# Retention between the products of the first of four d_ff passes, instead of ahead of all products

## The chip, the cores and the metric

One core of one Trainium2 chip. Times are device microseconds of one execution; a kernel is run several times and the median is quoted. Engines: PE is TensorE, PEld its weight loads, DVE is VectorE, ACT is ScalarE, POOL is GpSimd, SP is SyncE, whose queue (SPq) issues nearly all DMAs.

A line of a profile's timeline reads: start and duration in us, engine, line of the program (L396), operation, what is written <- what is read, shapes, xcount. Brackets give the engine's idle time before it and what ended it; "<-issue" means that the profile shows no releaser. "Evacuation" is the copy or addition that takes a product's result out of PSUM, the accumulator memory.

## The reference

Retention (attention with a decay in place of the softmax) makes x, and a two-layer block with the activation `h * erf(softplus(h))` follows. Everything is float32, except the weights, which come as float64 and are rounded in the kernel.

```python
batch, n_heads, seq, head_dim = (8, 8, 576, 64)        # q, k, v
n_tokens, d_model, d_ff = (4608, 512, 2048)            # w_in: 512 x 2048, w_out: 2048 x 512

scores = scale * np.matmul(q, k.transpose(0, 1, 3, 2))
Dmat = np.where(rel >= 0, gamma[:, None, None] ** rel[None, :, :], 0.0)
attn_out = np.matmul(scores * Dmat, v)
x = attn_out.transpose(0, 2, 1, 3).reshape(B * S, H * D)

h = x @ w_in
sp = np.maximum(h, 0.0) + np.log1p(np.exp(-np.abs(h)))
return (h * erf(sp)) @ w_out
```

## The kernel before

It works in two parts. Part one goes through 40 pieces of up to 128 tokens (8 batches of five, the fifth of 64 tokens). Each piece has three stages on TensorE: transposes of q and k; scores; outputs, with a running state `kv` that carries earlier pieces of the batch. The result x goes to DRAM in nine chunks of 512 tokens. In the same part all 32 float64 weight tiles are rounded to float32, on ScalarE, VectorE and GpSimd in turn, and "sums" of weight blocks are made.

The sums are there because both matrix products are done with seven block products in place of eight (Strassen's method in Winograd's form): sums of blocks of the weights (S1 to S4, T1 to T4) and of x or g, seven products, sums of the results. One product in the text below is one call of `product` or `multiply1` for one group of columns: four float32 matmuls, eight matmul instructions in the trace.

```python
        for i in range(n_p + 2):                      # part one
            if i < n_p:
                transposes(i)
            if 0 <= i - 1 < n_p:
                scores(i - 1)
            if i >= 2:
                store((b * S + s0) // TCH)
                outputs(i - 2)
            round_weights(-(-len(todo) * (i + 1) // (n_p - 2)))
        store(n_ch)
    ...
    for c in range(n_ch):                             # part two, chunk by chunk
        for g in range(n_g):                          # four groups of d_ff
            middle_products(c, g)                     # S2, S3, S1
            if g > 0:
                finish_group(c, g - 1)
            if g + 1 < n_g:
                first_products(c, g + 1)              # A11, A12
            ...
            last_products(c, g)                       # S4, A22
            serf(c, g)
        ...                                           # 28 products by w_out, accumulated in PSUM over g
        load_x(c + 1)
        ...
```

The rounding of a weight tile is the same in both kernels:

```python
        nc.scalar.activation(a_f, high_f, AF.Abs)
        nc.scalar.mul(out=r_f, in_=low, mul=2.0**-52)
        nc.vector.tensor_scalar(...)                  # four VectorE operations
        ...
        nc.gpsimd.tensor_tensor(out=r_f, in0=high_f, in1=r_f, op=ALU.mult)
        nc.gpsimd.tensor_tensor(out=a_f, in0=a_f, in1=r_f, op=ALU.add)
        load_weights()
        if sums:
            sums(...)                                 # four VectorE adds; they wait for GpSimd
```

## Time and profile before

| | |
|---|---|
| time | 1186.71 us median of 3 runs (1184.98 to 1187.42) |
| part one, to the first product | 298 us, TensorE busy 217 us, clock 0.82 |
| part two | 889 us, TensorE busy 875 us, clock 1.00 |
| busy over the span | PE 92%, DVE 43%, ACT 34%, POOL 10% |

Read the table by halves. In part two TensorE is idle for 14 of 889 us, so little but fewer or cheaper products can help there. In part one it is idle for 81 of 298 us, and its clock is lowered. The lines that show this stand in the prediction.

### The profile page before, as it was taken

Reading aid. Unit: us, or ns where it says so; the run is one execution under the profiler, and the core shown is the slowest. Engines: PE = TensorE matmul, PEld = TensorE weight load, DVE = VectorE, ACT = ScalarE, POOL = GpSimd, SP = SyncE. Lnnn points to the kernel's source line nnn. Section 1 sums busy time; section 2 is a strip of 40 time slices with the busy share of each in tenths; the row PEclk is TensorE's granted clock in tenths of the full one; section 3 lists DMA queues with packets and bytes.
Section 4 is the critical chain, followed back from the end, with each engine's and each line's share of the span. In section 5 each row is a group of like instructions: output and inputs, shape, how many; then the busy total and the mean of one; then the engine's idle time right before and its main releaser. Section 6 shows DMA issues by size and latency. Waiting matters only on the chain.

```text
span 1186.5 us, 14961 instructions
## 1 busy us (share of the span) xinstructions
PE 1092.2 (92%) x6400; PEld 950.7 (80%) x6400; DVE 510.6 (43%) x721; ACT 403.2 (34%) x533; POOL 120.4 (10%) x110
## 2 busy tenths in 40 slices
PE   4778678876999999999999999999999999999998
PEld 3666567665888888888888888888888888888887
DVE  3766665664462164056045317315504622721540
ACT  3343344331361162055036016205404602520630
POOL 3544444341000000000000000000000000000000
PEclk8888887778999999999999999999999999999999
DMA  9878977972010000001001000100000000000000
GB/s 256 183 184 194 225 194 191 223 177 97 12 36 1 36 1 36 36 1 36 16 20 36 1 36 1 36 36 1 36 18 19 36 1 36 21 15 36 1 1 36
DMA packets 124818, 75.76 MB, mean 64 GB/s; under 512 B 113616, under 2 KB 113616, under 8 KB 122320
## 3 DMA queue, kind: packets, MB, share of 16 engines
q1 hardware_dynamic: 124608, 73.41, 24.1%
q10 hardware_dynamic: 144, 1.40, 0.3%
q8 instruction: 50, 0.82, 0.3%
q14 instruction: 16, 0.13, 0.0%
HBM read 55.92 MB, written 18.87 MB: 63 GB/s over the span
## 4 chain that ended last, share of the span: by engine, by line
PE 75%; DMA 7%; ACT 5%; DVE 5%; POOL 3%; issue 2%; SPq 1%; ACTq 0%; POOLq 0%; DVEq 0%
PE acc_a L362 21%; PE oa L432 20%; PE acc_g L362 10%; PE og L432 10%; PE acc_e L362 5%; ACT e L410 2%; PE s L245 2%; DMA raw_k<-in_k_dram 2%; DMA raw_q<-in_q_dram 2%; PE o L261 2%; DVE g L143 1%; PE oe L432 1%; DMA raw_v<-in_v_dram 1%; PE o L271 1%; POOL wraw L198 1%
## 5 line engine op out<-in xcount | busy, mean ns | idle before, releaser
L432 PE MATMUL oa<-wb,s 128*128 128x256 f32 x864 | 191.0, 379 | 0.7 <-ACT osb L477 0.7
L432 PEld LDWEIGHTS oa<-wb,s 128*128 128x128 f32 x864 | 164.1, 190 | 23.3 <-ACT osb L477 1.1
L362 PE MATMUL acc_a<-x,wa 128*128 128x256 f32 x576 | 138.0, 383 | 7.9 <-DMA x<-xd 7.9
L362 PE MATMUL acc_a<-xs,wa 128*128 128x256 f32 x576 | 136.1, 379 | 0.0
L362 PE MATMUL acc_g<-xs,wa 128*128 128x256 f32 x576 | 136.1, 379 | 0.0
L143 DVE TENSOR_TENSOR osb<-og,osb 128x512 f32<-128x512 f32 x18 | 12.5, 692 | 284.2 <-ACT osb L477 166.4
L362 PEld LDWEIGHTS acc_a<-x,wa 128*128 128x128 f32 x576 | 110.4, 192 | 23.2 <-DMA x<-xd 8.0
L432 PE MATMUL og<-wb,g 128*128 128x256 f32 x576 | 127.3, 379 | 0.0
L362 PEld LDWEIGHTS acc_a<-xs,wa 128*128 128x128 f32 x576 | 109.4, 190 | 14.9
L362 PEld LDWEIGHTS acc_g<-xs,wa 128*128 128x128 f32 x576 | 109.4, 190 | 14.9
L432 PEld LDWEIGHTS og<-wb,g 128*128 128x128 f32 x576 | 109.4, 190 | 14.9
L410 ACT ACT_TABLE_LOAD x72 | 92.4, 1283 | 67.5 <-DVE g L143 66.9
L143 DVE TENSOR_TENSOR g<-g,e 128x1024 f32<-128x1024 f32 x72 | 84.7, 1218 | 52.0 <-ACT e L410 52.0
L245 PE MATMUL s<-qT,kT 64*128 64x128 f32 (+1 forms) x640 | 58.7, 339 | 23.7 <-DVE sT L143 23.6
L245 PEld LDWEIGHTS s<-qT,kT 64*128 64x128 f32 (+1 forms) x640 | 49.7, 236 | 31.8 <-DVE sT L143 26.5
L432 PE MATMUL oa<-wb,g 128*128 128x256 f32 x288 | 67.5, 382 | 7.9 <-DVE g L143 7.9
L410 ACT ACTIVATE e<-g 128x1024 f32<-128x1024 f32 x72 | 72.1, 1049 | 1.0 <-DVE g L143 0.6
L410 ACT ACTIVATE e<-e 128x1024 f32<-128x1024 f32 x72 | 72.1, 1049 | 0.4
L432 PEld LDWEIGHTS oa<-wb,g 128*128 128x128 f32 x288 | 54.0, 190 | 18.5 <-DVE g L143 11.5
L362 PE MATMUL acc_e<-x,wa 128*128 128x256 f32 x288 | 68.4, 380 | 0.0
L394 DVE COPY g<-acc_a 128x512 f32<-128x512 f32 x36 | 24.9, 692 | 99.4 <-PE acc_a L362 99.4
L382 ACT COPY g<-acc_a 128x512 f32<-128x512 f32 x36 | 20.7, 576 | 137.0 <-PE acc_a L362 137.0
(58 smaller groups left out, 1167.3 us busy)
## 6 DMA issues: line engine op xcount, KB each, us to landing
xd<-xT SPq DMA_DIRECT2D x9, 1024.0 KB, 6.2
x<-xd SPq DMA_DIRECT2D x9, 1024.0 KB, 4.8
out_dram<-osb SPq DMA_DIRECT2D x18, 512.0 KB, 2.8
raw_q<-in_q_dram SPq DMA_DIRECT2D x32, 256.0 KB, 5.1
raw_k<-in_k_dram SPq DMA_DIRECT2D x32, 256.0 KB, 6.0
raw_v<-in_v_dram SPq DMA_DIRECT2D x32, 256.0 KB, 6.3
wraw<-in_moe_w_in_dram SPq DMA_DIRECT2D x16, 512.0 KB, 4.5
wraw<-in_moe_w_out_dram SPq DMA_DIRECT2D x16, 512.0 KB, 3.8
```

The costliest lines, as they stand in the source:

```text
L143: nc.vector.tensor_tensor(out=out, in0=in0, in1=in1, op=op)
L198: nc.gpsimd.tensor_tensor(out=r_f, in0=high_f, in1=r_f, op=ALU.mult)
L245: nc.tensor.matmul(ps[:n, e, p, :n], lhsT=t["kT"][r, p, :n], rhs=t["qT"][r, p, :n], start=True, stop=True)
L261: nc.tensor.matmul(o[e * D : (e + 1) * D, p, :n], lhsT=t["v"][:n, 2 * p + e, :], rhs=t["sT"][:n, e, p, :n], start=(p == 0), stop=(s0 == 0 ...
L271: nc.tensor.matmul(o[:, p, :n], lhsT=kept["state"][:, p, :], rhs=t["qT"][:, p, :n], start=False, stop=(p == NP - 1), skip_group_check=True,)
L362: nc.tensor.matmul(acc[:, j * TH : (j + 1) * TH], lhsT=wa[:, a, d, f : f + P], rhs=x[c][a][:, d, :], start=(start and j == 0 and d == 0), ...
L382: nc.scalar.copy(out=t["g1"][:, 0], in_=t["a"])
L394: nc.vector.tensor_copy(out=t["g2"][:, 1], in_=t["a"])
L410: nc.scalar.activation(t["e" + j], t["g" + j] if func == AF.Softplus else t["e" + j], func)
L432: nc.tensor.matmul(acc[:, tp, :], lhsT=left[:, j * TH + tp * P : j * TH + (tp + 1) * P], rhs=wb[:, a, g * GP + j, :], start=(start and g = ...
```

## The change

The intent is to fill part one's idle TensorE with products. The d_ff columns are taken in four passes, and each pass goes through all nine chunks, so that only a quarter of the weights is needed to begin. The retention stages of chunk n+2 run between the products of chunk n in the first pass. The weights of a pass are rounded one pass ahead, one tile per chunk. The price: outputs are sums over passes, so each chunk's partial output goes to DRAM and comes back, and x is loaded and its block sums are made in every pass.

```diff
-    wa = const.tile([P, 7, 2, D_FF // 2], FP32, name="wa")
-    wb = const.tile([P, 7, n_fp, OH], FP32, name="wb")
+    wpool = ctx.enter_context(tc.tile_pool(name="wpool", bufs=2))      # weights of two passes
+    od = [dram.tile([P, 2, 2, D_MODEL], FP32, tag="od", name="od") for _ in range(n_ch)]
...
+    def attend(upto):                       # the next retention stages, in order
+        while done[0] < min(upto, len(stages)):
+            of, i = stages[done[0]]
+            of(i)
+            done[0] += 1
...
+        def begin(self):
+            self.o = opool.tile([P, 2, 2, D_MODEL], FP32, tag="o", name="o")
+            if self.g > 0:
+                nc.sync.dma_start(out=self.o, in_=od[self.c])
...
+    order = [(g, c) for g in range(n_g) for c in range(n_ch)]
...
+    weigh_values(0)
+    while done[0] < stages_for(TCH):
+        attend(done[0] + 1)
+        if done[0] % 2 == 1 and rounded[0] < 7:
+            round_weights()
+    sums_x(0, 0)
+    def run(steps):                         # a retention stage behind every product
+        for _ in steps:
+            attend(done[0] + 1)
+    run(firsts[0].first())
+    run(firsts[0].middle())
+    run(firsts[0].last())
+    firsts[0].erf()
+    round_weights()
+    attend(stages_for(2 * TCH))
...
+    for b, nxt in zip(blocks[1:], blocks[2:] + [None]):
+        n = order.index((b.g, b.c))
+        if isinstance(b, First):            # products by w_in
+            seconds[n - 1].begin()
+            if n + 1 < n_s and order[n + 1][0] > 0:
+                load_x(*order[n + 1])
+            run(b.middle())                 # S2, S3, S1
+            firsts[n - 1].sums()
+            run(seconds[n - 1].first())     # B11, B21
+            run(b.last())                   # S4, A22
+        elif n + 2 < n_s:                   # products by w_out
+            f = firsts[n + 1]
+            steps = b.middle()              # T2, T3, T1
+            for step, _ in enumerate(steps):
+                attend(done[0] + 1)
+                if step == 0:
+                    f.erf()
+            if n + 2 < n_ch:
+                attend(stages_for((n + 3) * TCH))
+            sums_x(*order[n + 2])
+            run(nxt.first())                # A11, A12
+            f.multiply()
+            run(b.last())                   # B22, T4
+            round_weights()
...
```

Cut here: the constants (the decay by position is split in two factors, so the scaling of outputs is four operations a piece and not one), the classes First and Second with the same seven products as before, the scores in two PSUM tiles.

## The prediction

> **What bounds the kernel now.** I read the page's 40 slices first, then the busy time of the two halves, then the timeline inside each half. Three rows of the slices (TensorE busy in tenths, its granted clock in tenths, DMA busy in tenths) show two programs one after the other:
>
> ```profile
> PE   4778678876999999999999999999999999999998
> PEclk8888887778999999999999999999999999999999
> DMA  9878977972010000001001000100000000000000
> ```
>
> Ten slices of retention with TensorE part idle, its clock at 0.7 to 0.8 and the DMA nearly full; then thirty of the MoE block with TensorE full and the DMA empty. The busy time by stretch (columns PE, PEld, DVE, ACT, POOL, clock, DMA share, GB/s) gives the boundary, 298 us:
>
> ```profile
> 0.00:298.00 298.00, 216.95 (x2368) 184.00 (x2368) 172.26 (x262) 105.14 (x209) 120.42 (x110) 0.82 0.82 192
> 298.00:1187.00 889.00, 875.27 (x4032) 766.68 (x4032) 338.38 (x459) 298.01 (x324) 0.00 (x0) 1.00 0.06 21
> ```
>
> The second half is bound by TensorE: 875 of 889 us at clock 1.00, VectorE (DVE) 38% busy. The timeline there gives the unit of the whole argument, one product of eight matmul instructions, and the VectorE steps behind it:
>
> ```profile
> 600.71 1.89 PE L362 MATMUL acc_a<-xs,wa 128*128 128x256 f32 x8
> 602.44 1.89 PE L362 MATMUL acc_a<-x,wa 128*128 128x256 f32 x8
> 602.64 0.69 DVE L394 COPY g<-acc_a 128x512 f32<-128x512 f32 x1 [2.76 <-PE acc_a L362]
> 603.37 0.69 DVE L143 TENSOR_TENSOR g<-acc_g,g 128x512 f32<-128x512 f32 x1
> 604.17 1.89 PE L362 MATMUL acc_e<-x,wa 128*128 128x256 f32 x8
> 616.06 2.35 DVE L143 TENSOR_TENSOR g<-g,e 128x1024 f32<-128x1024 f32 x2
> ```
>
> Products start 1.727 us apart (600.71, 602.44, 604.17). 4032 / 8 = 504 products, so 504 x 1.727 = 870 us is the floor of that half, and only about 19 us of it is anything else. The first half, by contrast, waits: for q, k, v loads, for VectorE, and on a slow clock. Where it does run freely, near its end, the timeline shows what retention costs TensorE at full clock:
>
> ```profile
> 270.16 0.66 PE L232 MATMUL pt_q<-ident,raw_q 128*128 128x128 f32 x4
> 270.65 0.60 PE L232 MATMUL pt_k<-ident,raw_k 128*128 128x128 f32 x4
> 275.16 2.08 PE L245 MATMUL s<-qT,kT 64*128 64x128 f32 x16 [3.90 <-DVE sT L143]
> 281.05 1.11 PE L245 MATMUL s<-qT,kT 64*128 64x128 f32 x15
> 282.09 1.09 PE L261 MATMUL o<-sT,raw_v 128*64 128x128 f32 x16
> 283.11 1.16 PE L271 MATMUL o<-qT,state 128*128 128x128 f32 x8
> 284.20 0.69 PE L285 MATMUL kv<-raw_v,raw_k 128*64 128x64 f32 x16
> 298.10 3.78 PE L362 MATMUL acc_a<-x,wa 128*128 128x256 f32 x8 [7.86 <-DMA x<-xd]
> ```
>
> By starts, a full piece takes 0.49 + 0.56 + 1.04 + 1.02 + 1.09 + 0.61 = 4.8 us, against 298 / 40 = 7.4 us for a piece as it ran. The scores at 275.16, after a wait of 3.90 us, took 2.08 us where 1.11 is the full-clock time; the first product, after 7.86 us, took 3.78.
>
> **What the Trainium skill says.** "TensorE: Matmul & The Clock Gate", Part 1, has the clock fall to half after an idle window of about 3.4 us; the two pairs above agree (2.08 for 1.11, 3.78 for 1.89). So retention put between dense products should run at full clock. "ScalarE: Activation LUTs", What ACT_TABLE_LOAD costs, gives about 1283 ns for a load; this trace has 72 of mean 1283 ns, and the count stays 72. "VectorE: DVE Perf Modes", The TRN2 errata, gives (N+151)/0.96 ns for an fp32 tensor-tensor op; this trace agrees at 512 (691 to 692 ns). At 128 it gives 0.29 us, an estimate, for the new per-head scaling ops, of which this trace has none. "DMA: Bandwidth & Descriptors", Why small descriptors are slow, says small ones lose bandwidth; here 113616 of 124818 packets are under 512 B, almost all q, k, v, and the slices above are DMA-full while they load.
>
> **The change part by part.** The instruction counts come from the built program. TensorE's matmuls are the same in number and shape: 504 products, 40 pieces of retention. What changes is order.
>
> 1. Retention moves between the first pass's products. 32 full pieces x 4.8, less 8 x 1.09 for the pieces that start a batch and have no state product, plus 8 short pieces x about 2.9 (from their rows at 280.5 to 290) = 168 us of TensorE at full clock, in place of a 298 us stretch.
> 2. A start remains: the first chunk needs pieces 0 to 3 done and piece 4 transposed, with 7 of 32 weight tiles rounded beside them. In the trace before, piece 3's kv product ends near 47 us. The constants shrink from 2728 to 700 columns, about 1 MB less, but more weights are wanted early. I take 45 us, in which four of forty pieces (16 us of TensorE at full clock) get done.
> 3. So TensorE has 870 + 168 - 16 = 1022 us left after 45: 1067 us if nothing ever waits.
> 4. Between products 7 and 8 of the first chunk, three pieces must run without products between them. At 7.4 instead of 4.8 us a piece: +8 us.
> 5. VectorE gets heavier. Partial outputs are summed through DRAM: per chunk and later pass 7 adds of 0.69 us into the output tile; before, 7 such steps (4 of them on ScalarE) served four groups. The x sums, 4 x 0.69, run 36 times instead of 9. Per chunk of 14 products (24.2 us): 5 evacuations 3.5, two multiplies 2.4, sums 2.6, x sums 2.6, output adds 4.8 = 15.9 us, 66% busy. That fits, but VectorE works in order. From product T1's end: two adds, four x sums, one add, two multiplies, two adds = 0.72 + 0.69 + 2.54 + 0.70 + 2.37 + 1.42 = 8.4 us; TensorE next needs the last of these after five products, 8.6 us. Hardly covered: I put 0.2 us on each of 27 chunks, 5 us.
> 6. In 16 chunks of passes 2 and 3 (and in 8 of the first) one weight tile is rounded right at that point. Its four ops (0.43 + 0.43 + 0.69 + 0.43, about 2.1 us with gaps) go ahead of the copy that product S1 waits for: 8.5 + 2.1 + 0.7 = 11.3 us against 10.4 covered, about 1 us. In four of the 16 the tile's sums follow, and these wait for GpSimd (1.1 + 1.3 us) and then take 2.6 more: about 6 us. 12 x 1 + 4 x 6 = 36 us.
> 7. In the first pass a chunk has 24.2 + 4.4 pieces x 4.2 = 43 us of TensorE. VectorE has 15 + 4.4 x 3.0 (masks now in two ops of 0.69, scaling in four ops of 0.29, state add) + 3.8 for weights = 32 us, 75%. A retention stage is needed two products and one stage later, about 4.5 us, and VectorE's blocks of 2.4 to 2.75 us fit inside with little over. I put 2.5 us on each of 8 chunks and 4 us on the two with weight sums: 28 us.
> 8. Weight-load conflicts where the matmul shape changes, 240 times: the rows show gaps of 0 to 0.2 us only now and then. 8 us.
> 9. The end: no product is left to hide the last Softplus, Erf and multiplies behind, and the last partial output must come back by DMA (1 MB took 4.8 us for x). 6 us.
>
> DMA: a later chunk moves 1 MB x, 1 MB partials in, 1 MB out and at times 0.5 MB weights in 24 us, some 145 GB/s; the retention half ran 192 on average with small packets. Hidden, I expect.
>
> Sum: 45 + 1022 + 8 + 5 + 36 + 28 + 8 + 6 = **1158 us**, 2.4% faster.
>
> **The rivals.** First, TensorE stays full throughout (steps 5 to 8 nearly nothing): about 1085 to 1100. For it: ScalarE is below 40%, two accumulators alternate, and chunks already evacuate behind products without loss. Against: 75% of VectorE in strict order, where one late op stops TensorE. Second, VectorE becomes the real bound of the first pass: if scaling ops and GpSimd contention (the "wa" sums took 1113 ns instead of 692 beside GpSimd) bring it to 90%, the first pass costs 430 to 450 us and not 350 to 390; and once TensorE waits over 3 us its clock halves too. About 1190 to 1220. Third, DMA: the partial tile's load queues behind the reload of a weight buffer, which waits for GpSimd, and so arrives when product T2 is about to need its accumulator; 1 to 2 us on each of 27 chunks, +30 to 50 us. The trace speaks neither way.
>
> **Range and chances.** The certain part is 1067. The waits total 91 and rest on orderings that I walked by hand; I allow 40 to 140. **Predicted 1158, range 1105 to 1205.** The 2% line is at 1163, close above my number: faster 0.54, within 2% 0.39, slower 0.07.
>
> **What would show it.** Steps 1 and 3: clock near 1.0 and TensorE above 90% from about 50 us on; a transposition group of four about 0.5 us. Step 2: first "a" product near 45 us. Steps 5 and 6: TensorE idle before "a" products, released by VectorE, in bursts of 1 and 6 us that vanish in the last pass, which rounds no weights. Step 7: VectorE 70 to 80% in the first pass, and a pass of about 380 us. I am wrong if the first pass runs at a clock of 0.8, if later passes without rounding exceed 24.5 us a chunk, or if waits on DMA show up on VectorE.

## The result, and the profile after

The changed kernel took 1167.99 us (median of 4 runs, 1166.91 to 1172.49) against 1186.34 us of the kernel before in the same rounds. Ratios here are the mean time of one kernel's runs over that of the other's runs of the same rounds, so not quite the ratio of the medians: 0.9853, 95% interval 0.9825 to 0.9881. That is 1.5% faster, inside the predicted range, 10 us above the predicted number and on the other side of the 2% line.

The slices of the changed kernel's page (busy tenths of PE and DVE, PE's clock):

```profile
PE   6679999999999998998999799989998999999996
DVE  5756566666576575766566566666775565665654
PEclk8888999999999999999999899999999999999998
```

The slow retention half is gone: from the fourth slice on TensorE is nearly full, and from the fifth its clock is up, even while retention runs, to slice 14. Busy time by stretch (columns PE, PEld, DVE, ACT, POOL, clock, DMA share, GB/s); I cut at the first product, the second chunk's first product, the end of retention (just behind the ninth chunk's first product) and the end of rounding:

```profile
0.00:49.30 49.30, 28.21 (x256) 23.50 (x256) 28.55 (x54) 15.31 (x27) 18.91 (x22) 0.83 0.79 192
49.30:100.60 51.30, 39.33 (x356) 32.03 (x353) 28.74 (x57) 14.72 (x22) 13.47 (x12) 0.87 0.58 132
100.60:408.00 307.40, 304.97 (x2595) 253.52 (x2592) 199.79 (x411) 101.56 (x153) 44.90 (x41) 1.00 0.48 124
408.00:914.00 506.00, 469.24 (x2101) 403.57 (x2100) 328.26 (x503) 165.57 (x188) 42.73 (x36) 0.98 0.34 129
914.00:1165.10 251.10, 240.82 (x1104) 210.06 (x1102) 150.78 (x217) 74.97 (x78) 0.00 (x0) 0.99 0.33 122
```

In the third stretch, where retention and products are mixed, TensorE idles 2.4 of 307 us. It loses time in the first two (100 us, a third of it idle and the clock at 0.85) and in the fourth (37 us idle). The timeline inside the first pass shows mixed work at full clock, the retention stages as short as the fastest ones of before:

```profile
103.14 1.99 PE L371 MATMUL e<-x,wa 128*128 128x256 f32 x8
104.97 0.60 PE L243 MATMUL pt_q<-ident,raw_q 128*128 128x128 f32 x4
105.40 0.60 PE L243 MATMUL pt_k<-ident,raw_k 128*128 128x128 f32 x4
105.84 1.89 PE L371 MATMUL a<-xs,wa 128*128 128x256 f32 x8
```

The fourth stretch is best seen in one of its gaps. This is a chunk whose rounded tile completes a block, so that the four sums (`wa<-wa`, L91) follow the rounding:

```profile
544.28 1.89 PE L371 MATMUL a<-xs,wa 128*128 128x256 f32 x8
546.01 1.89 PE L371 MATMUL g<-xs,wa 128*128 128x256 f32 x8
547.15 0.43 DVE L201 TENSOR_SCALAR wraw<-wa 128x512 uint32<-128x512 uint32 x1
547.71 1.04 POOL L202 TENSOR_TENSOR wraw<-wraw 128x512 f32<-128x512 f32 x1 [22.42 <-issue]
548.83 1.27 POOL L203 TENSOR_TENSOR wa<-wa,wraw 128x512 f32<-128x512 f32 x1
550.14 2.62 DVE L91 TENSOR_TENSOR wa<-wa 128x512 f32<-128x512 f32 x4 [2.56 <-POOL wa L203]
552.67 0.68 DVE L396 COPY t<-a 128x512 f32<-128x512 f32 x1
553.41 3.78 PE L371 MATMUL a<-xs,wa 128*128 128x256 f32 x8 [5.51 <-DVE t L396]
```

Product S2 ended before 546.2, and S1 may only begin when VectorE has copied S2's result (L396). That copy takes 0.68 us, but it stands in VectorE's queue behind four sums, and the sums wait 2.56 us for GpSimd. TensorE idles 5.51 us, and then its clock is down: S1 takes 3.78 us where 1.89 is usual. In the stretch there are five such gaps (4.70, 5.51, 5.11, 5.51, 5.11 us), eleven of 0.33 us in chunks that round a tile without sums, and six of 0.25 to 1.62 us ahead of product T2. After 914 us, where no weights are left to round, the products follow each other without a gap until the last 30 us: 24.17 us a chunk, 14 x 1.727.

### The profile page after: what moved, and what is told of

Same layout as the page of the kernel before. It is cut to its first block, busy times and chain, and to the rows that moved or that the text cites. A ratio compares the mean times of both kernels' runs of the same rounds, so it can differ in the third digit from the quotient of the medians.

```text
span 1165.1 us, 15647 instructions
## 1 busy us (share of the span) xinstructions
PE 1082.6 (93%) x6400; PEld 922.7 (79%) x6400; DVE 736.1 (63%) x1240; ACT 372.1 (32%) x467; POOL 120.0 (10%) x110
## 5 line engine op out<-in xcount | busy, mean ns | idle before, releaser
L450 PE MATMUL a<-wb,s 128*128 128x256 f32 x864 | 208.1, 384 | 10.8 <-DVE o L91 10.8
L450 PEld LDWEIGHTS a<-wb,s 128*128 128x128 f32 x864 | 162.7, 191 | 37.2 <-DVE o L91 12.6
L371 PE MATMUL a<-xs,wa 128*128 128x256 f32 x576 | 147.4, 401 | 32.9 <-DVE t L396 31.4
L91 DVE TENSOR_TENSOR o<-a,o 128x512 f32<-128x512 f32 x108 | 74.4, 689 | 134.8 <-PE a L450 104.2
L371 PEld LDWEIGHTS a<-xs,wa 128*128 128x128 f32 x576 | 112.0, 199 | 56.1 <-DVE t L396 38.6
L371 PE MATMUL a<-x,wa 128*128 128x256 f32 x576 | 137.3, 381 | 0.0
L371 PE MATMUL g<-xs,wa 128*128 128x256 f32 x576 | 137.1, 381 | 0.0
L371 PEld LDWEIGHTS g<-xs,wa 128*128 128x128 f32 x576 | 108.2, 190 | 14.9
L371 PEld LDWEIGHTS a<-x,wa 128*128 128x128 f32 x576 | 108.1, 190 | 15.0
L91 DVE TENSOR_TENSOR t<-t,s 128x1024 f32<-128x1024 f32 x72 | 85.9, 1234 | 0.0
L91 DVE TENSOR_TENSOR t<-g,t 128x512 f32<-128x512 f32 x72 | 49.7, 690 | 43.9 <-PE g L371 42.6
```

The source lines that it names most:

```text
L91: nc.vector.tensor_tensor(out=out, in0=in0, in1=in1, op=op)
L371: nc.tensor.matmul(acc[:, j * TH : (j + 1) * TH], lhsT=weights["wa", self.g][:, a, d, j * P : (j + 1) * P], rhs=x[self.g, self.c][a][:, d, :],
L450: nc.tensor.matmul(acc[:, tp, :], lhsT=left[:, j * TH + tp * P : j * TH + (tp + 1) * P], rhs=weights["wb", self.g][:, b, j, :], start=(sta ...
```

## The experiments

Nine kernels ran, all with correct results. Each was timed beside the kernel before on its own chip (1185.76 to 1186.44 us there), in three rounds; "the change" below is 1168 us.

**Sums later.** Only the four sums move, one chunk on, behind the evacuation of product T2:

```diff
         if sums:
-            sums(*(w[:, i] for i in range(7)))
+            late.append(lambda: sums(*(w[:, i] for i in range(7))))
+            if g == 0:
+                finish_weights()                # the first pass's own weights: as before
...
                 if step == 0:
                     f.erf()
+                    finish_weights()
```

> Only the four sums of a finished weight block move, from behind the rounding (where they wait for GpSimd and stand ahead of the copy that product S1 needs) to one chunk later, behind the evacuation of product T2. Theory (in-order VectorE, not its load, makes the waits): the five TensorE gaps of 4.7 to 5.5 us before an S1 product and the half-clock product behind each (up to 1.9 us more) go: 26 + 8 = 34 us, so about 1134 us; the gaps of 0.33 us stay. Rival (VectorE is the bound of the later passes, so the same work stalls TensorE wherever it stands): the gaps reappear elsewhere, 1155 us or more.

It took 1130.99 us (1130.5 to 1134.05), ratio to before 0.9542 (0.9514 to 0.9571): 37 us less than the change, for the same work in another order. The fourth stretch, 408 to 914 us, in this run:

```profile
408.00:914.00 506.00, 492.52 (x2250) 424.76 (x2250) 347.54 (x530) 178.61 (x201) 41.80 (x36) 1.00 0.36 135
```

VectorE is now busier in this stretch (347.5 us against 328.3, since more chunks fit in it), and TensorE idles 13.5 us in place of 36.8. None of the five long gaps is left (nor one of 1.84 us at 297 us, in the first pass), and the clock is 1.00; the gaps of 0.33 us stay, as expected, and so do those before T2. So VectorE's load was not the bound; the place of the sums was.

**Reload behind the other loads.** Only the issue of the next weight load moves on SyncE's queue:

```diff
-        load_weights()
+        if g == 0:
+            load_weights()
...
                 load_x(*order[n + 1])
+            if len(words) < 4:
+                load_weights()
```

> Only the reload of the weight buffer moves on the SyncE queue: behind the loads of the partial tile and of x, not ahead of them. Theory (the queue stands still for the reload, which waits for GpSimd, and the partial tile comes 2 to 5 us late): the seven gaps of 0.25 to 1.6 us before T2 products go, 7 us in all, about 1161 us. Rival (the DMA is simply full in those microseconds): they stay, 1168 us.

(The change's trace has six such gaps, not seven; I had miscounted.) It took 1159.35 us (1157.99 to 1160.34), ratio 0.9772 (0.9749 to 0.9795): 8.6 us less. In the change, SyncE's queue stands until GpSimd has let go of the buffer that is to be reloaded, and the load of the partial tile (`o<-od`) is behind it:

```profile
581.17 1.28 POOL L203 TENSOR_TENSOR wb<-wb,wraw 128x512 f32<-128x512 f32 x1
582.48 0.55 SPq L170 DMA_DIRECT2D wraw<-in_moe_w_in_dram  x1
583.12 0.55 SPq L444 DMA_DIRECT2D o<-od  x1
590.35 0.69 DVE L91 TENSOR_TENSOR o<-a,o 128x512 f32<-128x512 f32 x1 [3.80 <-DMA o<-od]
591.10 1.99 PE L450 MATMUL a<-wb,s 128*128 128x256 f32 x8 [1.62 <-DVE o L91]
```

In the run with the reload behind, the same load of the same chunk is issued while GpSimd has not even begun, and VectorE's addition comes straight behind the sums of g:

```profile
577.70 0.60 SPq L445 DMA_DIRECT2D o<-od  x1
579.37 1.04 POOL L202 TENSOR_TENSOR wraw<-wraw 128x512 f32<-128x512 f32 x1 [30.05 <-issue]
585.18 0.69 DVE L91 TENSOR_TENSOR s<-t,s 128x512 f32<-128x512 f32 x1
585.78 0.68 DVE L91 TENSOR_TENSOR o<-a,o 128x512 f32<-128x512 f32 x1
```

The six gaps before T2 products in the fourth stretch are gone. The DMA had room; the queue's order was the cause.

**The change without its overlap.** All retention runs first, and x comes from DRAM in the first pass too:

```diff
+    attend(len(stages))
+    load_x(0, 0)
     sums_x(0, 0)
+    load_x(0, 1)
...
-            if n + 1 < n_s and order[n + 1][0] > 0:
+            if n + 1 < n_s:
```

> The change without its overlap: all retention runs first, x goes through DRAM also for the first pass, then the four passes, with rounding a pass ahead as in the change. Theory (the overlap is what gains, the passes cost): first product near 290 us, then 870 us of products, six waits for weight sums of 7 us each, 12 us of small gaps and 9 us at the end: about 1225 us, slower than both. Rival (the gain of the change is the rounding taken out of the retention half): about 1180 us or less.

It took 1226.57 us (1224.28 to 1229.7), ratio 1.0342 (1.0313 to 1.037). The total is as the theory had it, but two of its terms were off and cancelled. The first product began earlier, and a gap came that I had not counted, behind the rounding and sums of the first pass's last tile:

```profile
256.56 3.50 PE L371 MATMUL a<-x,wa 128*128 128x256 f32 x8 [8.29 <-DMA x<-xd]
286.46 3.75 PE L371 MATMUL a<-xs,wa 128*128 128x256 f32 x8 [11.54 <-DVE xs L91]
```

So there are three amounts. With seven weight tiles and not 32 rounded beside it, smaller constants and its stages in their new order, retention took 257 us to the first product and not 298; no run separates these three. The rest of this version, passes and all, took 964 us after its first product, where part two of the kernel before took 889. And the overlap itself is worth 1226.6 - 1168.0 = 58.6 us. The rival's point holds in part (41 us of the retention half went without any overlap), but its total does not.

**Two stages a product in the first chunk.**

```diff
-    run(firsts[0].first())
+    def run_two(steps):
+        for _ in steps:
+            attend(done[0] + 2)
+    run_two(firsts[0].first())
```

and so for `middle` and `last`.

> Two retention stages and not one behind each of the first chunk's seven products, so only one or two stages are left to run alone before the second chunk. Theory (14.2 us of stages took 28.9 us because each waits for the one before with nothing between): 8 us less, about 1160 us. Rival (VectorE and GpSimd set the pace of these stages, with the weight rounding among them): the waits move between the products, 1166 us or more.

It took 1172.28 us (1170.56 to 1172.83), ratio 0.988 (0.9856 to 0.9903): no gain, so my theory fell, and the waits moved as the rival had it. One of 4.13 us came inside the first chunk (at 58.79 us, where the change waits 1.46 and 0.66 us). The second chunk's first product did come earlier, at 91.57 us and not 100.60, and then TensorE waited again, at 102.20 us for 6.10 us. VectorE's own timeline in this run says why:

```profile
93.63 0.43 DVE L191 TENSOR_SCALAR wb<-wb 128x512 f32<-128x512 f32 x1 [4.83 <-ACT wb L187]
98.59 2.72 DVE L91 TENSOR_TENSOR wb<-wb 128x512 f32<-128x512 f32 x3 [2.29 <-POOL wb L203]
101.23 0.87 DVE L91 TENSOR_TENSOR state<-kv,state 64x256 f32<-64x256 f32 x2
102.13 1.63 DVE L314 SCALAR_TENSOR_TENSOR x<-o,cst 128x64 f32<-128x64 f32 x8
```

The state and the scaled outputs of piece 8 (101.23 and 102.13) stand behind the rounding of the last tile of w_out and its sums, which wait for ScalarE and for GpSimd. That they hold TensorE is inferred here, since the profile gives its wait no releaser; the last run below tests it. As in the first experiment, weight sums that wait for GpSimd stand in front of work that TensorE needs.

**A shorter start.** With the sums later as above, only the four tiles of w_in are rounded ahead of the first product, and w_out's four inside the first chunk:

```diff
-        if done[0] % 2 == 1 and rounded[0] < 7:
+        if done[0] % 2 == 1 and rounded[0] < 4:
             round_weights()
+        if done[0] == 9:
+            finish_weights()
```

with one `round_weights()` behind each of `first`, `middle` and `last` of the first chunk.

> The sums moved as in the first run, and at the start only the four tiles of the first weight are rounded before the first product, their sums behind the next scores; the four of the second weight are rounded inside the first chunk. Theory (the start waits 9.2 us for VectorE, which waits for GpSimd's rounding, not for data): the first product at 40 to 42 us and not 49, 8 us less than the sums alone: about 1123 us. Rival (the loads of q, k, v and weights set the start): the first product stays near 48 us, 1130 us.

It took 1123.3 us (1120.97 to 1126.86), ratio 0.9473 (0.9452 to 0.9494): 7.7 us less than the sums alone. The first product came at 42.72 us, a little later than expected. The wait for VectorE ahead of piece 2's outputs, in the run with the sums alone and in this one:

```profile
38.05 2.47 PE L274 MATMUL o<-sT,raw_v 128*64 128x128 f32 x16 [9.21 <-DVE sT L91]
31.13 2.47 PE L272 MATMUL o<-sT,raw_v 128*64 128x128 f32 x16 [3.29 <-DVE sT L91]
```

**All four together.** The edits are the sum of the four reorderings above (not of the run without overlap).

> Sums later, reload behind the other loads, shorter start, two stages a product in the first chunk. Theory (separate waits, each on its own): 37 + 8.6 us as measured, 8 for the start, and now also some 6 for the two stages a product, since the rounding that stood in their way is elsewhere: about 1108 us. Rival (each hides the next): 1120 us or more.

It took 1112.95 us (1110.7 to 1114.78), ratio 0.9382 (0.9365 to 0.9399). That lies between the two: 1123.3 less 8.6 for the reload would be 1114.7, so two stages a product again gave next to nothing. TensorE still waited 4.65 us before piece 10's transposes at 88 us and 3.36 us, for the x sums, at 94 us.

**Masking twice.** The change itself, with a loop over `(0, 1, 0, 1)` and not `range(2)` in the masking of scores, so that VectorE does this work twice.

> The change with the masking of the scores done twice (same values, twice the VectorE time: 80 more ops of 0.64 to 0.69 us, 6 us a chunk of the first pass). Prediction's step 7 (VectorE's blocks only just fit in the first pass, so waits grow at once): 20 to 50 us more. Rival (slack in the first pass is wide; TensorE idles 2.4 us in seven chunks): at most 8 us more, most of it at the start and in the stages that run alone, so 1170 to 1176 us.

It took 1182.88 us (1182.11 to 1187.51), ratio 0.997 (0.9954 to 0.9987), 15 us more than the change: above the rival's limit and below step 7's. The traces split it (the profiled run was the slowest of its four, 1187.51 us). The evacuation of the second chunk's first product came at 116.6 us and not 102.6, so 14 us were lost at the start, in the first chunk and where stages run alone; from there to the ninth chunk's first evacuation, 4.7 us more. In the 306 us from 102 to 408 VectorE went from 198.57 to 225.08 us busy, that is 65% to 74%, and TensorE stayed busy for 301.39 us (303.57 in the change):

```profile
102.00:408.00 306.00, 301.39 (x2594) 250.61 (x2594) 225.08 (x462) 94.71 (x147) 47.37 (x43) 0.98 0.50 125
```

This window still holds the last 14.6 us of the stages that run alone here. Cut from evacuation to evacuation (116.6 to 427.2 us), VectorE is 74% busy too, and TensorE idles 3.6 us against 2.4. So between products a VectorE at 74% costs TensorE little. Ahead of that, VectorE was busy 8.3 us longer (67.38 and not 59.11 us) and 14 us were lost: there its time counts in full and more.

**Rounding in halves.** All four together, plus: ScalarE's half of a rounding stays where it was, the VectorE and GpSimd half goes behind T2's evacuation in the next chunk, the sums behind B21's; and the last partial tile is fetched earlier (by the edit, ahead of five products, not three).

```diff
         nc.scalar.mul(out=r_f, in_=low, mul=2.0**-52)
+        if g > 0:
+            half.append(lambda: round_rest(...))
+        else:
+            round_rest(...)
...
         elif n + 1 < n_s:
+            seconds[n + 1].begin()
             firsts[n + 1].erf()
```

> As all four together, and the VectorE and GpSimd half of rounding moved behind T2's evacuation, the sums behind B21's; the last partial tile fetched three products earlier. Theory: the 16 gaps of 0.33 us go and 2 us at the end: 7 us under all four together, about 1101 us. Rival (VectorE is late elsewhere now): no gain or a few us more.

It took 1105.78 us (1101.98 to 1107.3), ratio 0.9318 (0.9298 to 0.9338): 7.2 us less. Of 506 us in the stretch from 408 to 914, TensorE was busy for 503.97. The gaps of 0.33 us are gone; three of 0.45 to 0.86 us stand before other products.

**Nothing in front of piece 8.** As that one, but the last two tiles of w_out are rounded elsewhere (one behind `middle`, one behind the second chunk's first products), and their sums no longer stand ahead of the second chunk's x sums.

```diff
     run_two(firsts[0].middle())
     round_weights()
+    round_weights()
     run_two(firsts[0].last())
-    round_weights()
     firsts[0].erf()
-    round_weights()
     attend(stages_for(2 * TCH))
-    finish_weights()
...
     firsts[0].multiply()
+    round_weights()
```

> As the best so far, but the rounding of the last two weight tiles of the first pass and their sums no longer stand on VectorE ahead of the scaling of piece 8 and the x sums of the second chunk. Theory (in the run with two stages a product, as in the change, the wait behind the first chunk is the weight block in front of VectorE's retention work): the gaps of 4.7 and 3.4 us near 90 us and the half-clock product behind the second go, 8 to 10 us: about 1097 us. Rival (the stages there are paced by their own chain or by loads): 1105 us as before.

It took 1096.82 us (1096.31 to 1097.05), ratio 0.9243 (0.9209 to 0.9276): 9.0 us less, and 7.6% under the kernel before. Both gaps near 90 us are gone (one of 1.39 us is left, at 96), which settles what the run with two stages a product left as inference: the rounding in that place made TensorE wait. The edit moves its ScalarE and GpSimd operations along with VectorE's, so the share of each isn't separated. The transposes of piece 10, in the run with rounding in halves and in this one:

```profile
89.38 1.08 PE L257 MATMUL pt_q<-ident,raw_q 128*128 128x128 f32 x4 [4.67 <-issue]
87.02 0.60 PE L257 MATMUL pt_q<-ident,raw_q 128*128 128x128 f32 x4
```

## Why the prediction was right or wrong

Right within its range: 1168 measured, 1158 predicted, 1105 to 1205. It leaned to "faster by over 2%", and the result was 1.5%. The mechanism held; sizes were off in both directions, and most of them cancelled. That the total came within 10 us is in part luck: step 7 was 26 us too high, and steps 2, 4 and 6 and the DMA were 28 us too low together. The differences below add up to about -3 us. Two amounts were in no step: the 4.8 us from the end of the last product (1160.3) to the end of the span (1165.1), and the 1.8 us by which the device time exceeds the span. The remaining 6 us or so stay open.

- **Steps 1 and 3, the certain part.** Held. A chunk of products takes 24.17 us where nothing waits, retention stages between products run at full clock, and TensorE is 99% busy in the mixed stretch. Only the forecast "above 90% from about 50 us on" came late: from 49 to 101 us it was 77% busy, at clock 0.87.
- **Step 2, the start.** 45 predicted, 49.3 measured. The longest wait, 9.15 us, was for VectorE: in it VectorE rounded a tile, waited 2.56 us for GpSimd and made sums for 3.46 us. The shorter start, with the same loads of q, k and v, took 6 us of it away.
- **Step 4, stages alone behind the first chunk.** 8 predicted, about 15 measured (28.9 us for stages that take 14.2 at full clock). I had priced them at the old pace of a piece and overlooked that the first pass's last rounding and sums are in front of them on VectorE; with these elsewhere the last run gained 9.0 us.
- **Step 5, VectorE's 8.4 against 8.6 us.** Held: no gaps there in the last pass, 0 and not 5 us.
- **Step 6, the rounding in later passes.** The mechanism is as told, GpSimd's part included. 36 predicted; measured, the five chunks with sums lose 37 us together against 24.17 us a chunk, and the eleven with a 0.33 us gap some 0.6 us each, about 44 in all. What I left out of this step is the clock: behind a gap of 5 us the next product takes 3.4 to 3.8 us and not 1.89. I also counted four such chunks where the stretch has five: a tile rounded near the end of the first pass leaves its gap in the second, at 446 us.
- **Step 7, the first pass. This is the step that failed.** "VectorE's blocks of 2.4 to 2.75 us fit inside with little over": 28 us predicted, 2.4 us of TensorE idle measured in seven chunks. VectorE was 65% busy, not 75%, and masking twice shows that even 74% leaves TensorE all but undisturbed. The term that was wrong is the wait per chunk: VectorE's blocks fitted, and the wait was 0.3 us a chunk on average, not 2.5 to 4. A percentage of busy time says little about in-order waits; here, which operation was in front of which said more.
- **Step 8.** 8 predicted. An estimate from 305.9 us between the evacuations of the second and the ninth chunk, less seven chunks of 24.17, less some 128 us of stages left at full clock, less 2.4 idle, leaves 6 to 7 us. No run separates it.
- **Step 9, the end.** 6 predicted; four gaps of 0.78, 1.91, 2.01 and 0.78 us and one half-clock product, 7 us.
- **The third rival, DMA.** Its mechanism was real and its size was not: 1 to 2 us on each of 27 chunks was feared, six gaps and 8.6 us were measured. One of the prediction's own signs of being wrong thus came true: a wait on DMA showed on VectorE (3.80 us for `o<-od`).

Why so large a change gained so little: overlap is worth 59 us and the lighter retention half 41 us, but the passes as ordered give back about 75 us (964 against 889 after the first product). (These come from medians and from single profiled runs, and add up to 25 us, not to the 18 measured.) Of that, 37 and 8.6 us went when nothing but the place of the sums and of the reload changed, so they are not the price of passes. With all the reorderings, start and first chunk included, 71 us came off the change's time for the same operations.

## What to carry to other kernels

When work is spread between the steps of a pipelined loop, look for its slowest hand-off (here VectorE to GpSimd and back) and put the second half of the work into a later step, so that the engine that other engines wait for never waits itself. Do the same on the DMA queue: a load that needs a buffer to come free goes behind the loads that need nothing. A wait of 5 us costs more than 5 us if TensorE's clock falls with it (here up to 1.9 us more).

## What the Trainium skill lacked or had wrong

- "TensorE: Matmul & The Clock Gate", Part 1, ties the lower clock to an idle window of about 3.4 us. In the change, gaps of 4.7 to 5.5 us did it each time (3.40 to 3.78 us for the next product), but shorter ones did it in some runs: a gap of 2.01 us, 5.7 us behind one of 1.91 us, was followed by a product of 3.65 us in the change, and one of 1.92 us by 3.23 us in the last run. In the run with the shorter start the same two gaps (1.91 and 2.00 us, 5.7 us apart) cost nothing (1.97 us), nor did a lone gap of 1.84 us in the change (1.99 us). What decides between these is not shown.
- "ScalarE: Activation LUTs", What ACT_TABLE_LOAD costs, adds a drain of about 1380 ns to the load's 1283 ns. These traces show the 1283 ns, with no room for a drain on either side of the load: the activation before it ends at 613.61 us, the load runs from 613.63 us for 1.28 us, and the next activation starts at 614.92 us (the kernel before).
- "VectorE: DVE Perf Modes", The TRN2 errata, gives, by its formula for an fp32 addition, 0.29 us at 128 elements (an estimate). The scaling operation (PSUM source, a scalar by pointer) took 344 ns on average, and four in a row 1.12 to 1.13 us, so 0.28 us each when they follow each other.
- "SBUF — State Buffer", SBUF: two separate sides, says that a GpSimd operation and a VectorE operation that uses two ports, or has two SBUF inputs (this only where the GpSimd operation reads SBUF), exclude each other on a shared port pair for a whole instruction. Nothing wrong here, and one number: in the change a VectorE operation that elsewhere takes 0.43 us began at 17.40 us beside a GpSimd operation (17.09 us, 1.42 us long) and took 1.40 us, to 0.29 us behind the other's end. The trace doesn't show which ports it used.
- No page that I read says what in-order queues do to a hand-off between VectorE and GpSimd: in the five chunks with sums the wait of 2.3 to 2.6 us was about a third of the 7.4 us lost in each, the rest was what stood behind it and the lowered clock.
